# Plain FFN tiles: the down product in three stages, weight sums in place, rows as four chains, a planner with longer vector operations

## The chip, the cores and the metric

One core of a Trainium2 chip. The metric is the device time of one execution in microseconds (us), the median of three runs. Engines: PE (matmul), DVE (vector), ACT (activation), POOL (GpSimd), SP (issues most DMAs).

## The reference

One block of a network on x of 4096 positions by 640 features, in float32. Mod vectors come from a condition c; a spectral mixer works on the layer norm of x; then comes a gated feed-forward part on the layer norm of the result:

```python
mod = (_silu(c) @ w_mod).reshape(c.shape[0], 6, 1, -1)
h = _layernorm(x, axis=-1) * (1 + ca) + sa
x = x + ga * _A_ref(h, A_w1, A_b1, A_w2, A_b2)     # rfft, two small complex layers, soft threshold, irfft
h = _layernorm(x, axis=-1) * (1 + cb) + sb
x = x + gb * _B_ref(h, B_w_gate, B_w_up, B_w_down)  # (silu(h @ w_gate) * (h @ w_up)) @ w_down, 640 -> 1728 -> 640
```

## The kernel before

**Arithmetic.** To keep float32 accuracy, an operand is split into a high part (a rounded copy, ACT) and a low part (the rest, a subtraction on DVE), and a product is three matmuls: high by high, high by low, low by high.

**Phases.** The first 311 us are the mixer. What follows is the feed-forward part, over the 32 rows of 128 positions in six tiles (`TL`): two plain tiles of 4 rows (t = 0, 1) and four tiles of 6 rows (t = 2 to 5). The latter compute 2 x 2 blocks with seven products in place of eight (`seven`, `down7`); their sums of weights are made during the plain tiles and kept in DRAM (`td`, `wqd`).

**Stages of a plain tile.** The 1728 hidden features are six pairs of 256 (`NPR`), a half stage m and a small remainder s. `WG` lists the weight stages: g0, u0, s, g1, u1, g2, u2, ... g5, u5, m (gate and up of each pair), numbered n = 0 to 13. A weight stage is 30 matmuls of 128x512 into PSUM (`pg`). `down(t, p)` multiplies the hidden values (tiles `a`) by `w_down` (tiles `wq`) into PSUM banks `pd`, for each row g and half hf of the 640 features, and DVE adds each bank to the residual (`add_row`, the row L2246). The residual of tile 1 and later is loaded from DRAM (`x2d`).

**Weights.** `prep_w` splits gate and up weights (`r` to `wb`: high on ACT, low on DVE, in two pieces of 512 and 768 columns). `sum_w` makes the sums for the seven products (`ts` on POOL, `wt`, stored to `td`). `prep_wd` loads a pair of `w_down` (`wdr`, tag `wd`), multiplies it by the gate vector on POOL (L1483) and splits it (`wq`, low at L1494). `prep_wt` makes the four sums of the `w_down` blocks on POOL (`tr`), splits them (`tq`) and stores them. `kept_at(p)` names the plain tile in which pair p is also summed and stored.

**Rows.** Every row of tiles 1 to 5 has to be finished a tile ahead: load (`cr`, `x`, `gt`), gate product on POOL (L1610), split (`chh` on ACT, `chl` on DVE, L1617), a DFT product on PE (`py`, L1627), residual and statistics on DVE, scales on POOL, normed row on ACT (`xn`, L1658). Two rows make a pair: PE transposes them (`pt`, L1690), ACT scales, and the split result goes to DRAM (`ho` to `hs`).

**What sets the order.** All of this is planned when the kernel is built. Every operation is a `Step` with an engine, a reckoned duration, what it depends on, and the buffers it takes and frees; steps stand in chains. PE's matmuls are emitted in their order, and after every 0.3 us of them (`slot`) `sweep` tries each chain and emits the steps whose inputs are due by the planner's clock. `EARLY` says how far ahead of its due time a step may be emitted, and "T" is a step on PE (DFT product or transpose). What a stage needs and is not emitted yet, `until` and `force` emit at once. Each engine then works its queue strictly in that order. Durations reckoned for DVE's split of a `w_down` tile, for a weight sum and a row's split, and for POOL's gate product:

```python
Step("V", 0.83, lambda f=f: low(f), (("wdhh", t, p, f),), ("wdf", t, p, f),
Step("V", 0.7, low, (("tsh", n, i),), ("tsl", n, i), free=(tag,) if i else ()),
Step("V", 0.83, low, (k("chh"),), k("chl"), free=("pc",))
Step("P", 1.62, gated, (k("cr"),), k("crg"))
```

Of the kernel before, what the change touches and what calls it, by code (L numbers as in the profile page):

```python
# [173 lines left out]
def body(tc, x, w1, b1, w2, b2, wg, wu, wd, c, wm, k_fa, k_tb, k_tx, k_bm, k_bx, k_ga, k_ge, k_id, out, dbg=None):  # L174
# [27 lines left out]
    with ExitStack() as top:  # L202
# [836 lines left out]
        with ExitStack() as ff:  # L1039
# [22 lines left out]
            STG7 = [x for n, (k, p) in enumerate(WG) for x in [("w", n)] + [("d", p // 2 - 1)] * (k == "g" and p in (2, 4))]  # L1062
            STG7.append(("d", NPR // 2 - 1))

# [11 lines left out]
            LAT = 0.12  # L1076
            now = [0.0]
# [4 lines left out]
            EARLY = {"A": 0.0, "V": 0.3, "P": 0.3, "S": 0.3, "G": 0.3, "T": -1.5, "N": 0.0}  # L1082
# [5 lines left out]
            half1 = {"wd": 1, "wq": 4, "tr": 1, "tq": 2, "sg": 4, "hx": 5, "rb0": 1, "ra0": 1, "ra1": 1}  # L1088
# [9 lines left out]
            class Chain:  # L1098
# [11 lines left out]
                def at(self):  # L1110
                    st = self.steps[0]
                    t = 0.0
                    if st.e == "T" and not any(room[f"p{q}"] for q in (1, 2, 3)):
                        return None
                    for d in st.deps:
                        if d not in done:
                            return None
                        t = max(t, done[d])
                    for tag in st.use:
                        if not room.get(tag):  # L1120
                            return None
                        t = max(t, min(room[tag]))
                    return t

                def run(self):
# [10 lines left out]
                    elif e == "N":  # L1136
                        end = t
                    elif e in "SG":
                        q = "S" if e == "S" else "P"
                        issue = max(free[q], now[0], t) + (0.45 if e == "S" else 0.6)  # L1140
                        st.f()
                        free[q] = issue
                        free["D"] = max(free["D"], issue + 0.9) + 1.1 * st.n
                        end = free["D"] + 1.3
                    else:
                        start = max(free[e], now[0], t)
                        st.f()
                        free[e] = start + st.n
                        end = free[e] + LAT
# [35 lines left out]
            def sweep():  # L1185
                held = False
                for c in tails + chains:
                    if c in rows:

                        if held:  # L1190
                            continue
                        tries(c)
                        held = len(c.steps) > 0
# [12 lines left out]
            def force(c):  # L1206
                st = c.steps[0]
                for d in st.deps:
                    until(d)
                for tag in st.use:  # L1210
                    make_room(tag)
                c.run()

            def until(key):
                while key not in done:
                    force(owner[key])
# [3 lines left out]
            def make_room(tag):  # L1220
                while not room[tag]:
                    for c in tails + chains:
                        k = next((k for k, st in enumerate(c.steps) if tag in st.free), None)
                        if k is not None and (c.steps[k].e != "x"):
                            force(c)
                            break
                    else:
# [29 lines left out]
            def second_half():  # L1257
                nonlocal hq
                while tails:
                    while tails[0].steps:  # L1260
                        force(tails[0])
                    tails.pop(0)
                half.close()
                halves.pop(0)
                first.clear()
# [56 lines left out]
            def free_bank(qs):  # L1322
                while not any(room[f"p{q}"] for q in qs):
                    force(next(c for c in rows if c.steps and c.steps[0].e in "AV"))
# [11 lines left out]
            rows = [chain() for _ in range(NT)]  # L1336
# [129 lines left out]
            def kept_at(p):  # L1466
                return 0 if p < NPR // 2 else 1
# [4 lines left out]
            def prep_wd(t, p):  # L1472
# [15 lines left out]
                def high(f):  # L1488
                    wqs[t, p, f] = take("wq", [P, 2, 2, 320], F32R, 4, f"wq{t}_{p}_{f}")
# [29 lines left out]
            def prep_wt(p):  # L1519
                tr, tq = [], {}  # L1520

                def sub(j):
                    if j == 0:
                        tr.append(take("tr", [P, 4, 320], F32, 1, f"tr{p}"))
                    b11, b12, b21, b22 = (wdraw[p][:, f, 320 * e:320 * e + 320] for f in range(2) for e in range(2))
                    a, b = ((b12, b11), (b22, tr[0][:, 0]), (b22, b12), (b21, tr[0][:, 1]))[j]
                    pool.tensor_tensor(tr[0][:, j], a, b, op=OP.subtract)

                def high(i):
                    tq[i] = take("tq", [P, 2, 2, 320], F32R, 2, f"tq{p}_{i}")  # L1530
                    act.activation(tq[i][:, :, 0], tr[0][:, 2 * i:2 * i + 2], AF.Copy)

                def low(i):
                    dve.tensor_tensor(tq[i][:, :, 1], tr[0][:, 2 * i:2 * i + 2], f32(tq[i][:, :, 0]), op=OP.subtract)

                def store(i):
# [3 lines left out]
                            ("tr", p, j), ("tr",) if j == 0 else (), ("wd",) if j == 3 else ()) for j in range(4)]  # L1540
                for i in range(2):
                    out += [Step("A", 0.74, lambda i=i: high(i), (("tr", p, 2 * i), ("tr", p, 2 * i + 1)), ("tqh", p, i), ("tq",)),
                            Step("V", 0.83, lambda i=i: low(i), (("tqh", p, i),), ("tql", p, i), free=("tr",) if i else ()),
# [7 lines left out]
            DORD = ((1, 0), (2, 2), (6, 5), (7, 6), (5, 4), (4, 7), (3, 3))  # L1551
# [214 lines left out]
            def row_chain(t):  # L1766
# [157 lines left out]
            def finish0(t, n, f, pg):  # L1924
# [9 lines left out]
                else:  # L1934
                    tags, fc, sg = (f"a{2 * f}", f"a{2 * f + 1}"), 2 * p + f, sgs[f]
# [222 lines left out]
            def down(t, p):  # L2158
                G = 2 * TL[t][1]
                last = p == NPR - 1  # L2160
# [5 lines left out]
                for q in [p] + ([NPR] if last else []):  # L2166
# [3 lines left out]
                need(2 * p)  # L2170
                need(2 * p + 1)
# [6 lines left out]
                def seq(g, hf):  # L2178
                    q = []
                    for f in range(2):  # L2180
                        w = wqs[t, p, f]
                        l = [left(t, 2 * p + f, hl, g) for hl in range(2)]
# [12 lines left out]
                def put(g, hf, x):  # L2195
                    end = add_row(t, g, hf, x[0])
                    room[x[1]].append(end)
                    if last:
                        done["o", t, g, hf] = end

                def out(g):
                    H = TL[t][1]
                    outs.add([out_step(t, g, ("gx",) * ((g % H == H - 1) if t else 2 * (g == G - 1)))])

                for gs in ([(0, 1)] if last else [(0,)]) + [(g,) for g in range(2 if last else 1, G)]:
                    pd = {}
                    for g in gs:
                        for hf in range(2):
                            pd[g, hf] = any_bank(f"pd{t}_{p}_{g}_{hf}")
                            s = seq(g, hf)  # L2210
                            if last and len(gs) == 1:
                                s += tail_seq(g, hf)
                            for i, (l, m) in enumerate(s):
                                mm(pd[g, hf][0][:, :320], l, m, start=i == 0, stop=i == len(s) - 1 and not (last and len(gs) > 1))  # L2214
                            slot(0.147 * len(s))
                            if not last or len(gs) == 1:
                                put(g, hf, pd[g, hf])
                    if last and len(gs) > 1:
                        need(12)
                        for g in gs:  # L2220
                            for hf in range(2):
                                s = tail_seq(g, hf)
                                for i, (l, m) in enumerate(s):
                                    mm(pd[g, hf][0][:, :320], l, m, start=False, stop=i == 2)
                                slot(0.147 * 3)
                                put(g, hf, pd[g, hf])
                    if last:
                        for g in gs:
                            out(g)

                x = now[0] + 0.2
                for q in [p] + ([NPR] if last else []):
# [6 lines left out]
                for tag in ("a0", "a1", "a2", "a3") + (("ra0", "ra1", "rb0") if last else ()):  # L2239
# [165 lines left out]
            for t in range(NT):  # L2405
# [12 lines left out]
                if t:  # L2418
                    left_l.add(load_h(t))
                    x2_l.add(load_x2(t))  # L2420
                    rows[t].add(row_chain(t))

            for t in range(NT):

                for c in (sums, parts, down_s, down_t, outs):
                    chains.remove(c)
                    chains.insert(len(chains) - max(NT - 2 - t, 0), c)
                if t == NS:
                    second_half()
                for what, n in STG if t < NS else STG7:  # L2430
# [39 lines left out]
```

## Time and profile before

| | |
|---|---|
| median of 3 runs | 1451.06 us (1449.36 to 1453.6) |
| profiled execution | 1449.34 us, span 1447.5 us |
| PE, DVE, ACT, POOL busy | 97%, 75%, 53%, 41% of the span |
| DMA | 377.34 MB, mean 261 GB/s |

A row of the windows has the stretch, its length, then busy time and number of instructions of each engine, the clock that PE was granted (1.00 is full), and DMA. A row of the waits names who waited for whom, with the total, how often, and the longest. In the timeline a row has its start, its length and, in brackets, how long its engine was idle before and what ended that. A row of the groups has a line, the tiles written and read, the shape, the number of instructions, their busy time in us and the mean of one in ns, and the idle time before them. PE's matmuls overlap, so their own lengths say less than the distance of their starts.

### The profile page before, as it was taken

What the parts mean: (1) busy time and instruction counts of PE and PEld (TensorE: products, weight loads), DVE (VectorE), ACT (ScalarE), POOL (GpSimd) and SP (SyncE); (2) the same over time, 40 slices, a digit from 0 to 9 for tenths busy, and PEclk for the clock granted to TensorE, in tenths of its full rate; (3) what the DMA queues carried; (4) which work ended last, traced back from release to release, by engine and by line L of the source; (5) the groups of instructions that cost most, each with busy time, mean ns of one, the idle gap of its engine ahead of it and who ended that gap; (6) DMA issues with size and microseconds to landing.
All of it is one profiled execution on the core that took longest, in us unless ns stands there. A gap on an engine that the chain in (4) does not pass through costs nothing.

```text
span 1447.5 us, 23838 instructions
## 1 busy us (share of the span) xinstructions
PE 1397.2 (97%) x8410; PEld 1312.3 (91%) x8410; DVE 1079.9 (75%) x1911; ACT 763.7 (53%) x1542; POOL 591.5 (41%) x681
## 2 busy tenths in 40 slices
PE   7899999998999999999999999999999999999998
PEld 2599999967889888799999999999999999999998
DVE  8979888879988878838797757776667667365654
ACT  6779999744554444536454437354254535152441
POOL 5500200146756565515354625346334525052341
PEclk9999999999999999999999999999999999999999
DMA  9866466658976878998878997867997676955634
GB/s 366 312 213 213 157 196 208 205 170 268 324 251 222 306 236 295 320 387 302 289 241 288 325 357 259 284 228 262 384 326 246 238 279 243 361 178 198 219 126 145
DMA packets 170873, 377.34 MB, mean 261 GB/s; under 512 B 22178, under 2 KB 81634, under 8 KB 168739
## 3 DMA queue, kind: packets, MB, share of 16 engines
q1 hardware_dynamic: 161650, 359.28, 71.4%
q0 software_dynamic: 6800, 13.93, 2.9%
q10 hardware_dynamic: 2304, 2.62, 0.5%
q8 instruction: 66, 1.08, 0.3%
q14 instruction: 53, 0.43, 0.1%
HBM read 269.48 MB, written 96.80 MB: 253 GB/s over the span
## 4 chain that ended last, share of the span: by engine, by line
PE 59%; DVE 11%; issue 11%; DMA 8%; POOL 6%; ACT 3%; SPq 1%; DVEq 0%; POOLq 0%; ACTq 0%
PE pc L2289 8%; PE pw L1985 7%; PE pw L1987 7%; PE pw L1986 7%; PE pe L2289 6%; PE pd L2214 3%; DVE wb L1382 2%; PE pw L1996 2%; PE pw L1998 2%; PE pw L1997 2%; PE pc L707 2%; PE pl L657 2%; DMA h<-hs 2%; PE pg L1910 1%; PE pg L1908 1%
## 5 line engine op out<-in xcount | busy, mean ns | idle before, releaser
L1382 DVE TENSOR_TENSOR wb<-r,wb 128x768 fp32r<-128x768 f32 (+3 forms) x170 | 159.5, 949 | 11.3 <-ACT wb L1375 11.2
L1985 PE MATMUL pw<-h,wt 128*128 128x384 f32 x412 | 140.8, 342 | 6.9 <-ACT s_x L2004 3.8
L2045 POOL TENSOR_TENSOR sg<-s_x,sg 128x384 f32<-128x384 f32 x24 | 29.3, 1219 | 281.5 <-DVE s_x L2011 281.4
L1987 PE MATMUL pw<-h,wt 128*128 128x384 f32 x412 | 138.4, 336 | 0.0
L1986 PE MATMUL pw<-h,wt 128*128 128x384 f32 x412 | 138.1, 335 | 0.0
L2289 PE MATMUL pc<-wq,L 128*128 128x320 f32 x846 | 132.5, 310 | 1.2 <-DMA wq<-wqd 1.2
L2065 DVE TENSOR_TENSOR L<-sg,L 128x384 fp32r<-128x384 f32 x144 | 102.4, 732 | 39.2 <-ACT L L2061 35.3
L2289 PEld LDWEIGHTS pc<-wq,L 128*128 128x128 f32 x846 | 126.2, 188 | 1.8 <-DVE x L2246 1.2
L1375 ACT ACTIVATE wb<-r 128x768 fp32r<-128x768 f32 (+3 forms) x168 | 104.4, 637 | 43.7 <-PE pw L1998 39.5
L1910 PE MATMUL pg<-ht,wb 128*128 128x512 f32 x260 | 102.5, 394 | 5.5 <-DVE wb L1382 5.5
L1985 PE MATMUL pw<-h,wb 128*128 128x384 f32 x312 | 104.6, 335 | 0.0
L1987 PE MATMUL pw<-h,wb 128*128 128x384 f32 x312 | 104.4, 335 | 0.0
L1986 PE MATMUL pw<-h,wb 128*128 128x384 f32 x312 | 104.4, 335 | 0.0
L1908 PE MATMUL pg<-ht,wb 128*128 128x512 f32 x260 | 103.2, 397 | 1.2 <-ACT sg L1930 0.9
L2289 PE MATMUL pe<-wq,L 128*128 128x320 f32 x648 | 102.1, 310 | 1.5 <-DVE s_v L2011 0.8
L1909 PE MATMUL pg<-ht,wb 128*128 128x512 f32 x260 | 102.1, 393 | 0.0
L2004 ACT ACTIVATE s_x<-pw 128x384 f32<-128x384 f32 x52 | 25.4, 489 | 144.5 <-PE pw L1987 144.2
L2289 PEld LDWEIGHTS pe<-wq,L 128*128 128x128 f32 x648 | 96.3, 188 | 2.5 <-DVE s_v L2011 1.4
L2056 POOL TENSOR_TENSOR sg<-sg,sg 128x384 f32<-128x384 f32 x72 | 86.6, 1203 | 24.0 <-DVE L L2065 15.5
L2214 PE MATMUL pd<-wq,a 128*128 128x320 f32 x620 | 95.1, 310 | 0.0
L2214 PEld LDWEIGHTS pd<-wq,a 128*128 128x128 f32 x620 | 92.2, 188 | 1.0
L2246 DVE TENSOR_TENSOR x<-x,pc 128x320 f32<-128x320 f32 x144 | 68.2, 483 | 28.8 <-PE pc L2289 25.9
(324 smaller groups left out, 3892.9 us busy)
## 6 DMA issues: line engine op xcount, KB each, us to landing
wq<-wqd SPq DMA_DIRECT2D x83, 640.0 KB, 6.7
wt<-td SPq DMA_DIRECT2D x103, 512.0 KB, 4.9
hs<-ho SPq DMA_DIRECT2D x52, 512.0 KB, 6.1
h<-hs SPq DMA_DIRECT2D x32, 768.0 KB, 8.1
td<-wt SPq DMA_DIRECT2D x25, 512.0 KB, 5.1
r<-in_B_w_gate_dram SPq DMA_DIRECT2D x24, 384.0 KB, 4.6
r<-in_B_w_up_dram SPq DMA_DIRECT2D x24, 384.0 KB, 3.5
xx<-tt SPq DMA_DIRECT2D x56, 160.0 KB, 3.3
```

The costliest lines, as they stand in the source:

```text
L1375: def high(ks, e=slice(0, c), copy=lambda o, i: act.activation(o, i, AF.Copy)):
L1382: dve.tensor_tensor(wbs[t, n][:, 1, ks, e], raw[t, n][:, ks, e], f32(wbs[t, n][:, 0, ks, e]), op=OP.subtract)
L1908: mm(b, wh, hh, start=(kk == 0), stop=False)
L1909: mm(b, wh, hl, start=False, stop=False)
L1910: mm(b, wl, hh, start=False, stop=(kk == 4))
L1985: mm(b, w(0, kp), a[:, kp, 0], start=start and kp == 0, stop=False, skip_group_check=not start)
L1986: mm(b, w(0, kp), a[:, kp, 1], start=False, stop=False, skip_group_check=not start)
L1987: mm(b, w(1, kp), a[:, kp, 0], start=False, stop=kp == 1, skip_group_check=not start)
L2056: pool.tensor_tensor(o, x, y, op=op)
L2065: dve.tensor_tensor(o[:, 1], raws[j], f32(o[:, 0]), op=OP.subtract)
L2214: mm(pd[g, hf][0][:, :320], l, m, start=i == 0, stop=i == len(s) - 1 and not (last and len(gs) > 1))
L2289: mm(o[:, :320], ls[q][:, x, k], w[:, q, y], start=start and q == 0 and n == 0, stop=q == 1 and n == 2, skip_group_check=not start)
```

## The change

- `down` takes two pairs at a time: three stages per plain tile, after g2, after g4 and at the end, 12 products per bank (14 in the last stage, and 17 with the m part) in place of 6 (8, and 11).
- The sums in `prep_wt` are written over the loaded weights, so the tile `tr` goes. Buffers: `wd` 2 (was 1), `wq` 6 (was 4), `tq` 1 (was 2). The `hx` tiles of the start hold the hidden values of odd pairs.
- `kept_at`: pairs 3 to 5 are summed and stored in tile 0, pairs 0 to 2 in tile 1 (it was the other way round).
- The rows of a tile are four chains (pair steps, first rows, second rows, loads) in place of one.
- The planner multiplies durations on DVE and POOL by `SLOW`, except a row's residual adds and statistics: 1.3 and 1.2 in the plain tiles, 1.15 and 1.13 after. A "T" step is emitted once its input has been due for 0.5 us, it was 1.5. `force`, `until` and `make_room` go by one function `advance`, which emits what is possible and looks for what stands in the way.

```diff
-            STG = []
-            for n, (k, p) in enumerate(WG):
-                STG.append(("w", n))
-                if k == "g" and p:
-                    STG.append(("d", p - 1))
-            STG.append(("d", NPR - 1))
+            STG = [x for n, (k, p) in enumerate(WG) for x in [("w", n)] + [("d", p // 2 - 1)] * (k == "g" and p in (2, 4))]
+            STG.append(("d", NPR // 2 - 1))
...
+            SLOW = {"V": 1.3, "P": 1.2}
...
-            EARLY = {"A": 0.0, "V": 0.3, "P": 0.3, "S": 0.3, "G": 0.3, "T": -1.5, "N": 0.0}
+            EARLY = {"A": 0.0, "V": 0.3, "P": 0.3, "S": 0.3, "G": 0.3, "T": -0.5, "N": 0.0}
...
-            half1 = {"wd": 1, "wq": 4, "tr": 1, "tq": 2, "sg": 4, "hx": 5, "rb0": 1, "ra0": 1, "ra1": 1}
+            half1 = {"wd": 2, "wq": 6, "tq": 1, "sg": 4, "hx": 5, "rb0": 1, "ra0": 1, "ra1": 1}
...
-                        free[e] = start + st.n
+                        free[e] = start + st.n * (SLOW.get(e, 1.0) if st.key[0] not in ("x2", "mv") else 1.0)
...
+                SLOW.update(V=1.15, P=1.13)
...
-            rows = [chain() for _ in range(NT)]
+            rows = [[chain() for _ in range(4)] for _ in range(NT)]
+            tile_of = {c: t for t in range(NT) for c in rows[t]}
...
-                return 0 if p < NPR // 2 else 1
+                return 0 if NPR // 2 <= p < NPR else 1
...
-                    a, b = ((b12, b11), (b22, tr[0][:, 0]), (b22, b12), (b21, tr[0][:, 1]))[j]
-                    pool.tensor_tensor(tr[0][:, j], a, b, op=OP.subtract)
+                    o, a, b = ((b11, b12, b11), (b12, b22, b12), (b22, b22, b11), (b21, b21, b22))[j]
+                    pool.tensor_tensor(o, a, b, op=OP.subtract)
...
-                out = row_load(r0)
...
-                for i, (a, b) in enumerate(ab):
-                    (a1, a2), (b1, b2) = row_steps(a), row_steps(b)
-                    out += a1 + row_load(b) + a2[:4] + b1 + a2[4:] + b2
-                    st = pair_steps(t, i)
-                    m = 9
-                    out += st[:m] + (row_load(ab[i + 1][0]) if i + 1 < H else []) + st[m:]
-                return out
+                one, loads = ([], []), []
+                for i, rs in enumerate(ab):
+                    for h, r in enumerate(rs):
+                        c, x, g = row_load(r)
+                        if i:
+                            c.deps = tuple(("py", q, 1) for q in ab[i - 1])
+                        loads += [c, x, g]
+                        a1, a2 = row_steps(r)
+                        one[h].extend(a1 + a2)
+                return [[st for i in range(H) for st in pair_steps(t, i)], *one, loads]
...
-                need(2 * p)
-                need(2 * p + 1)
+                for f in range(4 * pp, 4 * pp + 4):
+                    need(f)
```

How the order moves on DVE in the opening of tile 0, between the products of stage u0 and the weights of stage g1 (`sg` the product with the gate, `a` the low hidden part, `wq` a split of `w_down`, `wb_3` the weights of g1, `x` the adds of a row's DFT product, `tq` the split of a sum). Before:

```order
L1940 TENSOR_TENSOR sg_0_0_4052<-pg_1_0_4165,sg_0_0_4052 128x512
L1494 TENSOR_TENSOR wq_0_0_4063<-wdr_0_4053,wq_0_0_4063 128x2x320
L1494 TENSOR_TENSOR wq_0_1_4219<-wdr_0_4053,wq_0_1_4219 128x2x320
L1945 TENSOR_TENSOR a_0_0_1_4057<-sg_0_0_4052,a_0_0_0_4056 128x512
L1940 TENSOR_TENSOR sg_0_1_4163<-pg_1_1_4208,sg_0_1_4163 128x512
L1382 TENSOR_TENSOR wb_3_4246<-r_3_4182,wb_3_4246 128x512
L1631 TENSOR_TENSOR x_4049<-x_4049,py_0_4258 128x320
L1631 TENSOR_TENSOR x_4049<-x_4049,py_1_4262 128x320
L1945 TENSOR_TENSOR a_0_1_1_4059<-sg_0_1_4163,a_0_1_0_4058 128x512
L1534 TENSOR_TENSOR tq_0_4269<-tr_4233,tq_0_4269 128x2x320
L1382 TENSOR_TENSOR wb_3_4246<-r_3_4182,wb_3_4246 128x768
```

And DVE's rows in the same place after:

```order
L1951 TENSOR_TENSOR sg_0_0_4052<-pg_1_0_4173,sg_0_0_4052 128x512
L1640 TENSOR_TENSOR x_4049<-x_4049,py_0_4214 128x320
L1640 TENSOR_TENSOR x_4049<-x_4049,py_1_4218 128x320
L1502 TENSOR_TENSOR wq_0_0_4063<-wdr_0_4053,wq_0_0_4063 128x2x320
L1956 TENSOR_TENSOR a_0_0_1_4057<-sg_0_0_4052,a_0_0_0_4056 128x512
L1502 TENSOR_TENSOR wq_0_1_4238<-wdr_0_4053,wq_0_1_4238 128x2x320
L1951 TENSOR_TENSOR sg_0_1_4171<-pg_1_1_4209,sg_0_1_4171 128x512
L1390 TENSOR_TENSOR wb_3_4258<-r_3_4199,wb_3_4258 128x512
L1390 TENSOR_TENSOR wb_3_4258<-r_3_4199,wb_3_4258 128x768
```

The two pieces of `wb_3` now follow each other; the adds stand ahead of them, `a_0_1` behind, and `tq_0` is gone from here.

PE at the first row's DFT product in tile 0 (`pg_1` is stage u0, `pg_2` stage s, `py` the DFT product). Before, it stood after the ninth matmul of stage s:

```order
L1908 MATMUL pg_2_0_4237<-ht_2_4043,wb_2_4178 128x512
L1909 MATMUL pg_2_0_4237<-ht_2_4043,wb_2_4178 128x512
L1910 MATMUL pg_2_0_4237<-ht_2_4043,wb_2_4178 128x512
L1627 MATMUL py_0_4258<-chh_4186,gt_4040 128x320
L1627 MATMUL py_0_4258<-chl_4187,gt_4040 128x320
L1627 MATMUL py_0_4258<-chh_4186,gt_4040 128x320
```

On PE after, it stands behind the third matmul of u0's second half:

```order
L1919 MATMUL pg_1_1_4209<-ht_3_4041,wb_1_4037 128x512
L1920 MATMUL pg_1_1_4209<-ht_3_4041,wb_1_4037 128x512
L1921 MATMUL pg_1_1_4209<-ht_3_4041,wb_1_4037 128x512
L1636 MATMUL py_0_4214<-chh_4188,gt_4040 128x320
L1636 MATMUL py_0_4214<-chl_4189,gt_4040 128x320
L1636 MATMUL py_0_4214<-chh_4188,gt_4040 128x320
```

It has moved 21 matmuls towards the start: the other 12 of that half and 9 of stage s now follow it.

More of the change, by code (lines that the diff above doesn't have):

```diff
@@ L1118, in at @@
                         t = max(t, done[d])
-                    for tag in st.use:
-                        if not room.get(tag):
+                    for tag in set(st.use):
+                        n = st.use.count(tag)
+                        if len(room.get(tag, ())) < n:
                             return None
-                        t = max(t, min(room[tag]))
+                        t = max(t, sorted(room[tag])[n - 1])
                     return t
@@ L1258, in second_half @@
                 nonlocal hq
[L1259 to L1262, printed above, removed]
+                for c in [*tails, sums, parts, down_s, down_t]:
+                    while c.steps:
+                        force(c)
+                tails.clear()
                 half.close()
                 halves.pop(0)
+                SLOW.update(V=1.15, P=1.13)
                 first.clear()
@@ L1323, in free_bank @@
                 while not any(room[f"p{q}"] for q in qs):
-                    force(next(c for c in rows if c.steps and c.steps[0].e in "AV"))
+                    force(next(c for c in tile_of if c.steps and c.steps[0].e in "AV"))
                 return min((q for q in qs if room[f"p{q}"]), key=lambda q: min(room[f"p{q}"]))
@@ L1934, in finish0 @@
                 else:
-                    tags, fc, sg = (f"a{2 * f}", f"a{2 * f + 1}"), 2 * p + f, sgs[f]
+                    tags, fc, sg = ("hx", "hx") if p % 2 else (f"a{2 * f}", f"a{2 * f + 1}"), 2 * p + f, sgs[f]
                 for q in tags:
@@ L2164, in need @@
                     wait_pe(done["act", t, f])
-                for q in [p] + ([NPR] if last else []):
+                for q in ps:
                     for key in wd_keys(t, q):
@@ L2193, in tail_seq, with go @@
                     return [(l[0], v[:, hf, 0]), (l[0], v[:, hf, 1]), (l[1], v[:, hf, 0])]
[L2195 to L2203, printed above, removed]
+                def go(b, s, start, stop):
+                    for i, (l, m) in enumerate(s):
+                        mm(b[:, :320], l, m, start=start and i == 0, stop=stop and i == len(s) - 1)
+                        if i % 6 == 5:
+                            slot(0.147 * 6)
+                    slot(0.147 * (len(s) % 6))
                 for gs in ([(0, 1)] if last else [(0,)]) + [(g,) for g in range(2 if last else 1, G)]:
+                    part = last and len(gs) > 1
                     pd = {}
@@ L2238, in down @@
                             room["wq"].append(x)
-                for tag in ("a0", "a1", "a2", "a3") + (("ra0", "ra1", "rb0") if last else ()):
+                for tag in ("a0", "a1", "a2", "a3") + ("hx",) * 4 + (("ra0", "ra1", "rb0") if last else ()):
                     room[tag].append(x)
@@ L2420, in body @@
                     x2_l.add(load_x2(t))
-                    rows[t].add(row_chain(t))
+                    for c, steps in zip(rows[t], row_chains(t)):
+                        c.add(steps)
             for t in range(NT):
-                for c in (sums, parts, down_s, down_t, outs):
+                for c in (sums, parts, down_s, outs):
                     chains.remove(c)
-                    chains.insert(len(chains) - max(NT - 2 - t, 0), c)
+                    chains.insert(len(chains) - 4 * max(NT - 2 - t, 0), c)
                 if t == NS:
                     second_half()
-                for what, n in STG if t < NS else STG7:
+                for what, n in STG:
                     if what == "d":
```

115 lines of the change are left out of this document (59 added, 56 removed).

## The prediction

> **What bounds the kernel now.** I read the page first, then the windows, then PE's own waits by stage, then the timeline at the longest of them.
>
> ```profile
> span 1447.5 us, 23838 instructions
> PE 1397.2 (97%) x8410; PEld 1312.3 (91%) x8410; DVE 1079.9 (75%) x1911; ACT 763.7 (53%) x1542; POOL 591.5 (41%) x681
> ...
> core 0: us, PE busy (x) PEld busy (x) DVE busy (x) ACT busy (x) POOL busy (x), PEclk, DMA share, GB/s
> 326.00:352.00 26.00, 21.44 (x85) 16.55 (x86) 24.01 (x26) 13.08 (x24) 19.13 (x16) 0.87 0.78 255
> 342.00:349.00 7.00, 4.26 (x11) 3.12 (x11) 6.24 (x6) 3.18 (x6) 5.77 (x4) 0.53 0.60 182
> 352.00:476.00 124.00, 123.92 (x688) 111.47 (x687) 110.00 (x164) 62.98 (x110) 76.64 (x80) 1.00 0.80 274
> 476.00:634.00 158.00, 150.00 (x795) 131.86 (x794) 125.71 (x193) 71.85 (x128) 86.55 (x89) 1.00 0.85 299
> 634.00:1444.00 810.00, 797.45 (x4865) 787.87 (x4862) 543.74 (x957) 355.71 (x765) 330.11 (x335) 1.00 0.76 266
> ```
>
> PE sets the end, and the change leaves every matmul in place. So it can only take PE's gaps away, or add some. The five windows are the opening of tile 0, a half-clock stretch in it, the rest of tile 0, tile 1, and tiles 2 to 5. PE is idle for 26 − 21.44 = 4.6 us, 0.1, 8.0 and 12.6 us in the four that do not overlap: 25.2 us together. The half clock adds (1 − 0.53) × 7 = 3.3 us, of which a part lies under the wait named next. About 27 us, 1.9% of the span, is therefore the most that a new order can bring. Who keeps PE waiting (columns: in total, times, longest), in the opening, in tiles 0 and 1 after it, the three longest of tiles 2 to 5:
>
> ```profile
> PE pg L1910 <- DVE wb L1382: 4.1, 2, 2.7
> ...
> PE pt L1690 <- ACT xn L1658: 3.7, 2, 3.0
> PE py L1627 <- issue: 1.9, 1, 1.9
> PE pg L1910 <- DVE wb L1382: 1.4, 1, 1.4
> PE pd L2224 <- DVE a L1945: 0.8, 1, 0.8
> ...
> PE pw L1985 <- ACT s_x L2004: 3.8, 4, 2.0
> PE pw L1985 <- ACT s_v L2004: 1.5, 4, 0.6
> PE pw L1985 <- ACT s_y L2004: 1.3, 4, 0.5
> ```
>
> **Tile 0's opening.** Stage g1 of tile 0 (gate, pair 1) waits for the low part of its weights, `wb_3`. On DVE there stood, between the two pieces of it:
>
> ```profile
> 339.24 0.68 DVE L1382 TENSOR_TENSOR wb<-r,wb 128x512 fp32r<-128x512 f32 x1
> 339.84 0.87 DVE L1631 TENSOR_TENSOR x<-x,py 128x320 f32<-128x320 f32 x2
> 340.64 1.77 DVE L1945 TENSOR_TENSOR a<-sg,a 128x512 fp32r<-128x512 f32 x1
> 342.33 1.34 DVE L1534 TENSOR_TENSOR tq<-tr,tq 128x640 fp32r<-128x640 f32 x1
> 343.59 1.47 DVE L1382 TENSOR_TENSOR wb<-r,wb 128x768 fp32r<-128x768 f32 x1
> ```
>
> In the changed order both pieces are neighbours, the `tq` step has gone to pairs 3 to 5, and the `a` step stands behind. That takes 1.77 + 1.34 = 3.1 us from in front of the second piece (the two `x` adds stay ahead of it, only earlier), more than its wait of 2.7 us. One sum of weights (`wt_01`) also moves behind and the adds come in front, so the first piece is not later. I take the whole 4.1 us as gone. The wait overlaps the half clock: in 342 to 349 PE is busy for 4.26 us at 0.53, which costs 4.26 × 0.47 = 2.0 us. That goes too, if the waits caused it: −6.1 us.
>
> [...]
>
> Against it, the first DFT product `py` now stands 21 matmuls earlier on PE (shown with the change). Neighbouring matmuls start 0.23 us apart:
>
> ```profile
> 330.05 2.19 DVE L1617 TENSOR_TENSOR chl<-cr,chh 128x640 fp32r<-128x640 f32 x1
> ...
> 335.73 0.30 PE L1627 MATMUL py<-chh,gt 128*128 128x320 f32 x1
> ...
> 426.12 0.39 PE L1908 MATMUL pg<-ht,wb 128*128 128x512 f32 x1
> 426.35 0.40 PE L1909 MATMUL pg<-ht,wb 128*128 128x512 f32 x1
> ```
>
> Its input was ready at 332.24, 3.5 us ahead of its use. 21 × 0.23 = 4.8 us earlier means that PE waits 1.3 us; the input itself may come a little sooner or later (one `wb` step has moved in front of it). I take +1.5, between 0 and 2.5. Opening: −4.6 us.
>
> **Down in three stages.** The matmuls stay; half of the adds into the residual go.
>
> ```profile
> L2246 DVE TENSOR_TENSOR x<-x,pd 128x320 f32<-128x320 f32 x96 | 42.9, 475 | 7.6 <-DMA x<-x2d 3.9 <-PE pd L2214 3.5
> ...
> 513.92 0.49 DVE L2246 TENSOR_TENSOR x<-x,pd 128x320 f32<-128x320 f32 x1 [3.89 <-DMA x<-x2d]
> ...
> 515.91 0.38 PE L1627 MATMUL py<-chh,gt 128*128 128x320 f32 x1 [1.94 <-issue]
> ```
>
> 48 adds × 0.475 = 23 us less on DVE in 308 us of tiles 0 and 1. DVE is busy there for 0.80 to 0.92 of the time, beside PE, so this by itself is worth nothing; it gives room. But tile 1's first add waited 3.9 us for its residual `x2d`, held PSUM banks meanwhile, and PE stood still for 1.9 us. The first down stage now comes two weight stages later: 60 matmuls × 0.23 = 13.8 us, far past the 3.9. −1.9 us. In the last stage the four held banks take 14 products each ahead of the remainder, before 8, so the wait of 0.8 us for `a12` is covered: −0.8 us. The wider stages need `wq` and `a` buffers for two pairs; there are six `wq`, and the `hx` tiles serve the odd pairs. Nothing waits longer for these by the order.
>
> **Weight sums in place, two `wd` buffers.** The four subtractions, two splits and two stores per pair stay, on all their queues. What goes is the wait for a single `wd` buffer. The longest wait of tile 1 came from it:
>
> ```profile
> 576.40 3.56 POOL L1483 TENSOR_TENSOR wdr<-wdr,gbb 128x640 f32<-128x640 f32 x2 [4.72 <-DMA wdr<-in_B_w_down_dram]
> ...
> 581.37 0.92 ACT L1658 ACTIVATE xn<-x,nm_b,rs_b 128x640 f32<-128x640 f32 x1 [6.72 <-POOL nm_b L1649]
> 582.34 0.55 PE L1690 MATMUL pt<-idn,xn 128*128 128x128 f32 x3 [3.02 <-ACT xn L1658]
> ```
>
> POOL waited for the load with a row's scales queued behind. With a load ahead this should shrink; but the buffer is now also held until the last split. I take −2.0 of the 3.0, between 0 and −3.0. Pairs 0 to 2 are now prepared for storing in tile 1 and 3 to 5 in tile 0, so tile 1's opening gets what tile 0's loses. Its `wb` wait of 1.4 us stays, and I add 1.0 (0 to 3).
>
> **Four chains, the planner's longer operations, transposes nearer.** The planner now reckons 1.3 for DVE in tiles 0 and 1 (1.15 later) and lets PE come at 0.5 in place of 1.5 after an input is due. The first is closer to the trace: `wq` is entered at 0.83, `wt` at 0.70.
>
> ```profile
> L1494 DVE TENSOR_TENSOR wq<-wdr,wq 128x640 fp32r<-128x640 f32 x28 | 31.2, 1142 | 2.0 <-ACT wq L1490 1.8
> L1617 DVE TENSOR_TENSOR chl<-cr,chh 128x640 fp32r<-128x640 f32 x28 | 30.2, 1077 | 7.7 <-ACT chh L1614 7.7
> L1449 DVE TENSOR_TENSOR wt<-ts,wt 128x512 fp32r<-128x512 f32 x25 | 27.0, 1081 | 9.8 <-ACT wt L1445 9.8
> ```
>
> 1142/830 = 1.38, 1081/700 = 1.54, and `chl` 1077/830 = 1.30. The second takes 1.0 us of slack from each of 28 rows' DFTs and 14 transposes. What slack there was, once each in tiles 0, 2 and 4:
>
> ```profile
> 389.78 1.36 DVE L1617 TENSOR_TENSOR chl<-cr,chh 128x640 fp32r<-128x640 f32 x1
> 391.10 0.30 PE L1627 MATMUL py<-chh,gt 128*128 128x320 f32 x1
> ...
> 735.08 0.81 DVE L1617 TENSOR_TENSOR chl<-cr,chh 128x640 fp32r<-128x640 f32 x1
> 736.63 0.31 PE L1627 MATMUL py<-chh,gt 128*128 128x320 f32 x1
> ...
> 1127.15 0.82 DVE L1617 TENSOR_TENSOR chl<-cr,chh 128x640 fp32r<-128x640 f32 x1 [1.71 <-ACT chh L1614]
> 1130.00 0.31 PE L1627 MATMUL py<-chh,gt 128*128 128x320 f32 x1
> ```
>
> That is 0.0, 0.7 and 2.0 us. So a row in tiles 0 and 1 would wait a whole us longer, if nothing else changed; but its planned steps have grown as well, `chl` by 0.25, the gate product on POOL (entered at 1.62, factor 1.2) by 0.32, so about half is given back, and DVE is freer. I take +2.0 for the 18 places there (−2 to +9) and −1.0 for tiles 2 to 5 (−6 to +6): the waits for ACT's evacuations come from ACT stuck behind late inputs, which the truer factors should thin, while nearer products give some back.
>
> Sum: −4.6 − 1.9 − 0.8 − 2.0 + 1.0 + 2.0 − 1.0 = −7.3 us. The profiled execution took 1449.34 us (1447.5 of it span), so 1442.0; it stood 1.72 below the median of the three runs, so the time is **1443.8 us**.
>
> **The rivals.**
> - *Larger gain.* The truer factors also clear the ACT waits of tiles 2 to 5 (3.8 + 1.5 + 1.3 = 6.6) and the rows cost nothing (−2.0): 1443.8 − 6.6 + 1.0 − 2.0, so about 1436. For it: those waits are the largest there. Against: they fall beside `rest` and the keeping copies, whose order hardly moves.
> - *No change.* Half of the 12 us of removed waits returns elsewhere on DVE, as the same work stands before the same deadlines: tile 1's opening (3.0) and the rows (4.0) take back the 7: 1451.
> - *Slower.* The split rows and nearer products make row inputs the bound: with two rows at once on POOL and DVE, each of 42 places waits 0.5 us more than counted. +21 − 7.3 = +13.7, so about 1465. It decides from 7.3/42 = 0.17 us per place on. For it: the slack of 0.0 above. Against: 2.0 in the late tiles, and 23 us less on DVE.
>
> **How the numbers follow.** Forecast 0.43, larger gain 0.20, no change 0.19, slower 0.18. The forecast's own range is 1438 to 1448. A measurement of this kernel can tell about 0.3% (4.4 us) from no change. Faster by more, below 1446.7: the first two less the forecast's upper end, plus the lower end of no change, 0.62; slower by more, above 1455.4: 0.18; within: 0.20. The range of 1431 to 1461 takes in three cases and the near half of the slower one.
>
> **What would show it.** After: no `wb` wait over 1 us in tile 0's opening, and a granted clock of 1.00 at 342 to 349; no wait of the add for `x2d`; 48 adds; a wait of about 1.5 us at the first `py`. It is wrong if PE's waits on `chl` and `xn` add up to more than 10 us, or if the opening of tile 1 loses over 4.

## The result, and the profile after

The changed kernel takes 1433.89 us (median of four runs, 1431.21 to 1435.43) beside 1450.72 of the kernel before: a ratio of 0.988, 95% interval 0.986 to 0.990. The forecast was 1443.8, with a range of its own of 1438 to 1448: the direction was right, and the gain of 7.3 us was too small by about 10, so that the time lies below that range, nearest to the 1436 of the rival of the larger gain. The profiled executions differ by 18.1 us.

The head of the page after:

```profile
span 1429.4 us, 23767 instructions
PE 1389.7 (97%) x8410; PEld 1313.1 (92%) x8410; DVE 1061.5 (74%) x1863; ACT 762.1 (53%) x1542; POOL 594.9 (42%) x681
```

And the windows of the same stages. At 326.2 us the kernel before starts stage u0, and the changed one the last two products of g0. From there the borders have moved, tile 1 is now 475 to 623.5 and tiles 2 to 5 are 623.5 to 1426:

```profile
326.00:352.00 26.00, 23.47 (x105) 19.12 (x106) 23.23 (x30) 15.42 (x26) 12.83 (x12) 1.00 0.52 175
342.00:349.00 7.00, 6.18 (x28) 4.86 (x28) 6.51 (x8) 4.74 (x8) 5.14 (x4) 1.00 0.49 171
352.00:475.00 123.00, 121.51 (x675) 109.05 (x674) 105.46 (x143) 63.86 (x111) 90.27 (x90) 1.00 0.89 311
475.00:623.50 148.50, 148.20 (x796) 131.78 (x795) 113.59 (x163) 73.37 (x132) 84.25 (x85) 1.00 0.90 316
623.50:1426.00 802.50, 794.75 (x4858) 789.26 (x4856) 542.21 (x955) 350.52 (x758) 328.24 (x332) 1.00 0.77 265
```

PE's idle time in these four stretches was 25.2 us and is 2.5 + 1.5 + 0.3 + 7.8 = 12.1. Nearly all of tile 1's 8.0 is gone. The other 5 us lie in PE's busy time. The half clock of 342 to 349 is gone (0.53 before, 1.00 now), but tiles 2 to 5 have one of 3.4 us that they did not have (shown at the end), so the clock's share of the 5 us is small: by estimate 4.26 × 0.47 = 2.0 us went and 3.40 × 0.50 = 1.7 us came. The rest is pace: products follow each other a little closer (busy time over matmuls in tile 1: 148.20/796 = 0.186 us, before 150.00/795 = 0.189), and why is not read off here. Who keeps PE waiting now, in the opening (two rows), the rest of tile 0, tile 1, and tiles 2 to 5:

```profile
PE py L1636 <- DVE chl L1626: 2.3, 2, 1.5
PE pg L1871 <- DVE ht L1858: 1.2, 1, 1.2
...
PE py L1636 <- DMA gt<-in_k_ga_dram: 0.9, 1, 0.9
...
PE pt L1699 <- ACT xn L1667: 0.3, 1, 0.3
...
PE pw L1996 <- ACT s_x L2015: 2.1, 2, 1.3
PE pe L2333 <- DMA wq_-1_11807<-wqt: 2.0, 1, 2.0
PE pe L2333 <- DMA wq_-1_9451<-wqt: 1.4, 1, 1.4
PE pc L2293 <- DVE s_v L2022: 0.9, 1, 0.9
```

The opening's waits on `wb` are gone. The longest left there is the first DFT product's, on its `chl`, as the timeline shows (two rows of PE, then two of DVE); the two `wb` pieces of stage g1, at 337.78, now follow each other:

```profile
326.20 0.73 PE L1871 MATMUL pg<-ht,wb 128*128 128x512 f32 x2 [1.22 <-DVE ht L1858]
...
333.24 0.42 PE L1636 MATMUL py<-chl,gt 128*128 128x320 f32 x1 [1.51 <-DVE chl L1626]
...
331.85 1.34 DVE L1626 TENSOR_TENSOR chl<-cr,chh 128x640 fp32r<-128x640 f32 x1
...
337.78 1.61 DVE L1390 TENSOR_TENSOR wb<-r,wb 128x512 fp32r<-128x512 f32 x2
```

And the group of the adds of the plain tiles, 48 in place of 96, with no wait for `x2d` left:

```profile
L2250 DVE TENSOR_TENSOR x<-x,pd 128x320 f32<-128x320 f32 x48 | 22.6, 481 | 15.8 <-PE pd L2209 15.8
```

### The profile page after: what moved, and what is told of

Same layout as the page of the kernel before. It is cut to its first block, busy times and chain, and to the rows that moved or that the text cites. A ratio compares the mean times of both kernels' runs of the same rounds, so it can differ in the third digit from the quotient of the medians.

```text
span 1429.4 us, 23767 instructions
## 1 busy us (share of the span) xinstructions
PE 1389.7 (97%) x8410; PEld 1313.1 (92%) x8410; DVE 1061.5 (74%) x1863; ACT 762.1 (53%) x1542; POOL 594.9 (42%) x681
## 4 chain that ended last, share of the span: by engine, by line
PE 68%; DVE 3%; DMA 3%; issue 1%; ACT 1%; POOL 1%; SPq 0%; DVEq 0%; ACTq 0%; POOLq 0%
PE pw L1996 8%; PE pw L1998 8%; PE pw L1997 8%; PE pc L2293 8%; PE pe L2293 6%; PE pd L2209 6%; PE pg L1921 3%; PE pg L1919 3%; PE pg L1920 3%; PE pw L2009 2%; PE pw L2007 2%; PE pw L2008 2%; PE py L1636 2%; PE pf L2333 1%; PE pt L1699 1%
## 5 line engine op out<-in xcount | busy, mean ns | idle before, releaser
L2076 DVE TENSOR_TENSOR L<-sg,L 128x384 fp32r<-128x384 f32 x144 | 105.9, 753 | 30.7 <-ACT L L2072 29.9
L764 POOL DMA_DIRECT2D s<-co x28 | 15.5, 553 | 179.4 <-ACT co L763 179.4
```

Source lines behind the costliest of these rows:

```text
L2076: dve.tensor_tensor(o[:, 1], raws[j], f32(o[:, 0]), op=OP.subtract)
```

## Experiments

Ratios are to the kernel before on the same chips, with 95% intervals. Waits are those of PE.

### One part of the change undone

Planning factors off, everywhere (both edits) and in tiles 2 to 5 alone (the second edit):

```diff
-            SLOW = {"V": 1.3, "P": 1.2}
+            SLOW = {"V": 1.0, "P": 1.0}
-                SLOW.update(V=1.15, P=1.13)
+                SLOW.update(V=1.0, P=1.0)
```

> The changed kernel with the planner's factors back at 1.0 in both halves; all else stays. Theory P (the gain beyond the forecast comes from the truer durations, which place every step): most of the 17 us goes, 1444 to 1452 us, tile 1 longer by 5 us or more and tiles 2 to 5 by 4 or more. Theory W (it comes from the wide down stages and the room they give DVE in the plain tiles): 1433 to 1438. Theory C (the split row chains): 1433 to 1438.

> The changed kernel with the factors of the second half (tiles 2 to 5) at 1.0; tiles 0 and 1 keep 1.3 and 1.2 and their order. Theory P (truer durations bring the gain of tiles 2 to 5): plain tiles as after, tiles 2 to 5 longer by 7 us or more, 1441 or more, with the waits for ACT's evacuations back at 5 to 7 us. Rival L (tiles 2 to 5 gained by where the loads of the next tile's left operand happen to fall on SP's queue, not by the factor): no more than 4 us in those waits; the time moves only if waits on h appear.

Measured: 1469.7 us, 1.012 (1.010 to 1.014), and 1451.2, 0.999 (0.997 to 1.001). The waits after 320 us of the first:

```profile
PE py L1636 <- DVE chl L1626: 11.0, 7, 2.9
PE py L1636 <- DMA gt<-in_k_ga_dram: 8.6, 3, 4.6
```

And those of the second in tiles 2 to 5:

```profile
PE py L1636 <- DVE chl L1626: 7.6, 3, 3.5
PE pw L1996 <- ACT s_x L2015: 2.8, 3, 1.6
```

So the rows' products do come too early for their inputs when T is -0.5 and the durations are short: the slower rival's mechanism exists (11.0 + 8.6 = 19.6 us in the first run), and the factors are what keeps it away. In the second run the order of the plain tiles is that of the changed kernel, instruction by instruction, and the loss lies in tiles 2 to 5, which take 820.2 us in place of 802.4:

```profile
625.90:1446.10 820.20, 799.17 (x4857) 790.71 (x4856) 545.40 (x954) 352.68 (x758) 327.01 (x332) 1.00 0.74 259
```

Its waits for ACT's evacuations are 3.6 us there (2.8 on `s_x`, 0.8 on `s_v`), not the 5 to 7 that I expected.

T back at -1.5, and, in another run, one row chain per tile in place of four (its steps in their old sequence):

```diff
-... "T": -0.5,
+... "T": -1.5,
```

```diff
-            rows = [[chain() for _ in range(4)] for _ in range(NT)]
+            rows = [[chain()] for _ in range(NT)]
```

> The changed kernel with products of rows emitted 1.5 us after their input is due, as before, in place of 0.5. My prediction's term (the nearer products cost 2 us in the plain tiles and about nothing later): 1430 to 1433, a little faster than the changed kernel. Rival (rows that are ready earlier release the queues behind them, the nearer products are part of the gain): 1436 to 1442.

> The changed kernel with the rows of a tile as one chain again. Theory C (rows that run side by side stop queues from waiting for one row's loads and statistics): 1440 to 1450, with waits for the transposes' input back in tile 1. Theories P and W: 1433 to 1437.

Measured: 1454.1, 1.001 (0.999 to 1.002), and 1501.1, 1.035 (1.033 to 1.037). With T -1.5 the longest of PE's waits is

```profile
PE pw L2007 <- DMA h<-hs: 10.1, 2, 7.4
```

and in the timeline of SP, ahead of tile 3, the last load of `h` stands behind two `wq` loads that came 8 us after the issue before them:

```profile
837.34 0.80 SPq L1565 DMA_DIRECT2D wq<-wqd  x2
838.18 1.36 SPq L1808 DMA_DIRECT2D h<-hs  x1
```

With one chain PE waits, around the start of tile 2 (two rows, 641 us) and of tile 3 (880 us), for

```profile
PE pw L1994 <- DMA h<-hs: 26.1, 4, 11.4
PE pw L2005 <- DMA h<-hs: 7.0, 1, 7.0
...
PE pw L2005 <- DMA h<-hs: 11.3, 1, 11.3
```

Both lose at the border of two tiles, where the next tile's normed rows (`h`) are not loaded in time.

Down in six stages again (with four `wq` and two `tq` buffers):

> The changed kernel with the down product of the plain tiles in six stages again (wq 4, tq 2 buffers as before, wd 2, sums in place). Theory W: 1441 to 1450, tile 1 longer by 5 us or more, the wait of the adds for the loaded residual back (2 to 4 us), tiles 2 to 5 as after. Theories P and C: 1434 to 1438 (my two small terms, 1.9 and 0.8 us, come back).

Measured: 1454.4, 1.002 (1.001 to 1.003); waits of 5.8 us on `h` and 6.2 on `wb`. DVE's wait for `x2d` is back, 5.3 us, and PE waits 1.3 us behind these adds:

```profile
L2252 DVE TENSOR_TENSOR x<-x,pd 128x320 f32<-128x320 f32 x96 | 43.0, 478 | 16.5 <-PE pd L2211 10.9 <-DMA x<-x2d 5.3
```

Each part undone thus brings the time to that of the kernel before or above it, though their single terms in the prediction are 0 to 2 us; four of these five runs took longer than any range that I expected of them. That fits no sum of terms: either the parts need each other, or any change of the order costs what this order happens to save.

### The same kernels with the order drawn anew

One number of the planner moved by a hundredth re-draws the order without touching the work: `LAT`, the latency added to each step's end (0.12 in both kernels), or the factors of tiles 2 to 5 by 0.01, which leaves the order of the plain tiles as it is.

```diff
-            LAT = 0.12
+            LAT = 0.13
```

> The changed kernel with the second half's factors at 1.16 and 1.14 in place of 1.15 and 1.13: a nudge with no meaning, which moves some orders. Theory P: 1432 to 1437, since the durations are as true as before. Rival L: the time may move by 5 to 15 us either way, all of it in tiles 2 to 5 at the borders between tiles.

> The changed kernel with the planner's latency between engines at 0.13 in place of 0.12 us: a nudge of all tiles. If the gain belongs to the parts of the change: 1430 to 1438. If a part of it is where orders happen to fall: 1438 to 1455.

> The kernel before with the same nudge of the planner's latency, 0.13 in place of 0.12 us. If the kernel before is typical of its planner: 1447 to 1455. If its time is an accident of order as well: outside of that.

> The changed kernel with the planner's latency at 0.11 us. With 0.12 it took 1433.9 and with 0.13 1444.8. If the shown time is a lucky draw of a spread: 1436 to 1450. If 0.13 was the unlucky one: 1430 to 1436.

> The kernel before with the planner's latency at 0.11 us. With 0.12 it took 1451 to 1452, with 0.13 1481.5. If the shown time of before is a lucky draw: 1456 to 1485, with waits on h at the tile borders. If 0.13 was the exception: 1447 to 1456.

> The changed kernel with the planner's latency 0.14. Theory R: the rows of tile 3 end over 60 us ahead of its start, as in every draw of the changed kernel so far (68 to 77), no wait on h over 5 us, 1434 to 1452 us. If the 1433.9 of the shown order is a lucky draw, this one lies at 1443 to 1452 as 0.11 and 0.13 did; if it is typical, at 1434 to 1440.

> The kernel before with the planner's latency 0.14. Theory R: one chain leaves the rows' lead to the draw: either the lead of tile 3 is about 60 us and the time 1448 to 1456 (as with 0.11 and 0.12), or it is under 20 us and the time 1470 to 1485 (as with 0.13). Nothing between them. Rival D: time and lead go separate ways, so a time over 1465 with a lead over 50.

| order | before, us | ratio | changed, us | ratio |
|---|---|---|---|---|
| LAT 0.11 | 1451.5 | 0.999 (0.997 to 1.000) | 1450.9 | 0.999 (0.997 to 1.001) |
| LAT 0.12, as shown | 1450.7 | 1 | 1433.9 | 0.988 (0.986 to 0.990) |
| LAT 0.13 | 1481.5 | 1.021 (1.019 to 1.022) | 1444.8 | 0.995 (0.994 to 0.997) |
| LAT 0.14 | 1478.0 | 1.018 (1.015 to 1.020) | 1446.8 | 0.996 (0.994 to 0.999) |
| LAT 0.12, factors +0.01 | | | 1437.5 | 0.992 (0.990 to 0.994) |

All ratios are to the kernel before in its own order. The changed kernel's shown order is the best of its five. The mean of its four ratios over LAT is 0.9946, or 1443 us on the scale of the kernel before. With LAT 0.11 the two kernels do not differ; with 0.13 and 0.14 they differ by 37 and 31 us, mostly by what the kernel before loses (next section). Tile 1 shows what differs among the changed kernel's orders. In each of three other orders of the changed kernel, the window of it and then the longest of PE's waits in it. LAT 0.11:

```profile
484.20:639.80 155.60, 150.65 (x796) 133.63 (x795) 120.33 (x163) 73.31 (x132) 84.08 (x85) 0.98 0.89 307
```

```profile
PE py L1636 <- DVE chl L1626: 4.7, 1, 4.7
```

LAT 0.13:

```profile
473.90:630.00 156.10, 150.99 (x802) 133.80 (x800) 122.22 (x173) 74.85 (x136) 87.81 (x92) 0.99 0.89 305
```

```profile
PE pg L1921 <- DVE wb L1390: 3.5, 2, 2.6
```

LAT 0.14:

```profile
471.80:627.20 155.40, 149.67 (x800) 132.17 (x800) 122.23 (x172) 74.81 (x134) 85.27 (x90) 1.00 0.86 301
```

```profile
PE pt L1699 <- ACT xn L1667: 3.6, 2, 1.9
```

Three orders, three operands that come late, 5 to 6 us of idle PE each; the shown order has 0.3. The work of the whole kernel is the same.

### Why the kernel before loses 30 us in two of four orders

With LAT 0.13 and 0.14 the kernel before waits 25 us for `h`, at the starts of tiles 3 and 4. In SP's timeline of the kernel before, the last store of tile 3's rows (`hs`) and the first loads of `h` behind it:

```profile
779.15 0.62 SPq L1735 DMA_DIRECT2D hs<-ho  x1
802.04 1.36 SPq L1797 DMA_DIRECT2D h<-hs  x2
```

The same with LAT 0.13, and in PE's the wait that follows:

```profile
835.26 0.38 SPq L1735 DMA_DIRECT2D hs<-ho  x1
840.41 4.66 SPq L1797 DMA_DIRECT2D h<-hs  x6
...
859.59 0.69 PE L1996 MATMUL pw<-h,wb 128*128 128x384 f32 x1 [17.57 <-DMA h<-hs]
```

Tile 3 starts at 841.5 and 839.7. So the rows were done 62 us ahead of it in the one order, and 4 us ahead in the other (5 with LAT 0.14): one chain takes its three row pairs one after the other, and where the first pair comes some 40 us later (first store at 657 and 696), the third ends at the border. What delays the first pair stays open. Two tests. If SP's order were to blame, loading `h` ahead of the other loads, and without the planner's limit on waiting DMA work, would mend it:

```diff
-            gate, prep, wld, wtl, down_w, left_l, x2_l, sums, ... = [chain() ...]
+            gate, prep, left_l, wld, wtl, down_w, x2_l, sums, ... = [chain() ...]
```

> The nudged kernel before (latency 0.13, 1481.5 us), with the loads of the next tile's left operand tried ahead of the weight loads and without their limit on planned DMA work. Rival L (the nudge cost its 29 us at the tile borders, because those loads stand behind others on SP's queue): the 25.6 us of PE's waits on h fall below 5, 1450 to 1460. Otherwise (the rows are late, the loads only show it): 1470 or more, the wait stays on the stores of hs.

> The changed kernel with the same earlier loads of the left operand. It had no wait on h, so by rival L nothing is to be gained: 1431 to 1438, unless the weight loads behind come late (waits on wq of 2 to 5 us more, 1436 to 1440).

Measured: 1483.1, 1.019 (1.017 to 1.021), no better. Its longest waits:

```profile
PE pw L1996 <- DMA h<-hs: 19.8, 2, 18.2
PE pc L2289 <- DMA wq<-wqd: 11.3, 2, 7.5
```

The changed kernel gets worse by it, 1460.2, 1.004 (1.003 to 1.006), since the loads of `wq` now stand behind:

```profile
PE pc L2293 <- DMA wq<-wqd: 22.2, 3, 8.0
```

If SP's order were the cause, the first would have come to 1450 to 1460; it is not the cause there. If the single row chain is, four chains will mend it. They were put into the kernel before, with what the planner needs for them and nothing else of the change:

> The kernel before, with one part of the change alone: the rows of a tile as four chains in place of one. Theory R (four chains finish the rows of the next tile earlier, so that its lefts are there when it opens; this is the change's own gain, and a part of the 17 us): 1440 to 1450 us, no wait on h over 2 us, the last store of tile 3's rows over 62 us ahead of tile 3's start (62 in the kernel before, 77 in the changed one). Rival D (the parts gain only together, since each re-draws the order): 1452 to 1475, with waits of 3 to 11 us on chl that the slower planning factors would have taken away, as in the runs without those factors.

> The kernel before with the planner's latency 0.13 and four chains in place of one. With one chain and 0.13 the time was 1481.5 us, with 25.6 us of waits on h, and the last store of tile 3's rows was only 4 us ahead of tile 3's start. Theory R: the rows are early again, over 50 us ahead, the waits on h fall under 6 us, and the time is 1446 to 1462. Rival Q (SP's queue holds the loads of h): the waits on h stay over 15 us and the time is over 1470.

Measured: 1457.3, 1.002 (1.000 to 1.004), and at LAT 0.13 1453.8, 1.002 (1.000 to 1.004). In SP's timeline at LAT 0.13, the last store of tile 3's rows, and then the wait on `h`:

```profile
748.77 0.36 SPq L1747 DMA_DIRECT2D hs<-ho  x1
```

```profile
PE pw L2010 <- DMA h<-hs: 1.8, 1, 1.8
```

Tile 3 starts at 857.9 there, 109 us behind the store, and 28 us of the time are back. So for LAT 0.13 the late rows of one chain are shown as the cause of that loss, and four chains as a cure; with 0.14 the cure was not run. In the five orders of the changed kernel, all with four chains, the lead of tile 3's rows is 51 to 77 us (for LAT 0.14 I had expected over 60; it is 51). But where the rows were early anyhow, four chains alone gain nothing: the 1440 to 1450 of the first theory was wrong, and the rival's waits came, 6.4 us on `chl` and `gt`.

### The two halves

All of the planner's part (four chains, factors, T) in the kernel before, and all of it undone in the changed kernel:

> The kernel before with the whole planner's half of the change (four row chains, the slower planning factors, T -0.5) and the old work: down in six stages, one wd buffer, weight sums in tiles of their own, old places of the stored blocks. If the planner's half is what took the late operands away, the waits on chl and gt of the run with four chains alone (6.4 us) fall under 3 us and the time is 1440 to 1452. If the parts gain only together with the new stages, as the run with six stages in the changed kernel says (1454.4), it is 1452 to 1458.

> The changed kernel with the planner's half undone (one row chain, no planning factors, T -1.5): the new stages and the weight sums in place alone. If one chain is the risk (44.6 us of waits on h in the changed kernel with one chain and the other planner's parts kept), the time is 1470 to 1510 with waits on h over 15 us; if it was the clash of one chain with the new factors, 1445 to 1455 with waits on h under 6 us.

Measured: 1453.0, 1.002 (1.000 to 1.004), and 1455.7, 1.002 (1.000 to 1.004). With the planner's half alone the waits on `chl` are down to 1.0 us, but PE waits (after 320 us) for `h`, `wb` and `wq`:

```profile
PE pw L2012 <- DMA h<-hs: 6.2, 2, 4.0
PE pg L1926 <- DVE wb L1396: 3.7, 2, 3.2
PE pd L2230 <- DVE wq L1508: 2.0, 2, 1.0
...
PE pd L2230 <- ACT wq L1504: 1.7, 1, 1.7
```

With the stages alone it waits for `xn`, `chl` and `wb`:

```profile
PE pt L1699 <- ACT xn L1667: 4.7, 4, 2.1
PE py L1636 <- DVE chl L1626: 4.4, 4, 2.6
PE pg L1919 <- DVE wb L1390: 2.8, 4, 1.1
```

In the run without the planner's half `h` waits only 0.7 us. So one chain is not late in every order; beside the new factors it cost 1501 us in the one order that was run. Neither half gains in the order that it got; the two together gain 0.4 to 1.2% in four of the five orders run, and in the fifth (LAT 0.11) nothing that can be told from noise. No version run beats the changed kernel.

## Why the prediction was right in direction and wrong in size

Against its own terms, from 326 us on (a border is the first product of a tile):

| stretch | forecast | measured |
|---|---|---|
| opening of tile 0 | -4.6 | -4.5: 20 more matmuls between 326 and 352, at 23.47/105 = 0.22 us |
| rest of tile 0 | about +1 (half of the rows' +2.0) | +3.5: 1.4 of waits, 7 more matmuls (1.6), rest unassigned |
| tile 1 | -1.9 - 0.8 - 2.0 + 1.0 + 1 = -2.7 | -9.0: 157.3 to 148.3 |
| tiles 2 to 5 | -1.0 | -7.9: 810.3 to 802.4 |

- **Opening: right.** No `wb` wait, clock 1.00 at 342 to 349, and 1.51 us at the first `py` where +1.5 was taken; a second wait on `chl` there adds 0.8. The half clock went with the waits, so the sum was right to count its 2.0 us. The start of tile 0 came 1.7 us earlier and that was lost again to `ht` (1.2 on DVE, 1.2 on ACT).
- **x2d and a12: right in this order.** The waits of 3.9 (DVE), 1.9 and 0.8 us are gone, and with six stages in the changed kernel the one on `x2d` is back (5.3). In the kernel before with four chains, or with the planner's half, which have six stages too, it is not there: this wait hangs on the order as well.
- **Tile 1: the step that failed, by its size.** I kept its `wb` wait of 1.4, took 2.0 of 3.7 us on `xn`, and added 1.0 for the opening and 1 for the rows. In the shown order of these only 0.3 us on `xn` is left: PE's idle time fell by 7.7 of 8.0, and the pace gave 1.3 more, together 6.3 us beyond the forecast. With LAT 0.11, 0.13 and 0.14 tile 1 takes 155.4 to 156.1, a gain of 1.2 to 1.9 where I forecast 2.7. With the factors 0.01 higher it is 148.3 again, but that is the same order of the plain tiles run once more and no further draw.
- **Tiles 2 to 5: the other one.** Forecast -1.0, from -6 to +6. The waits on ACT fell from 6.6 to 2.3, those on `h` (1.3) went; PE's waits there fell by 4.7 in all (12.3 to 7.6), and the rest is pace and a few matmuls less in the stretch (4858, before 4865). That the ACT waits would fall is what the rival of the larger gain (1436) said, which I gave 0.20. Its cause, the truer factors, is not shown: without them in these tiles the ACT waits are 3.6, still 3.0 less than before. What the factors do there is keep the rows' inputs in time (without them 7.6 on `chl`), and the tiles take 820.2 without them. The reason against the rival, that the order there "hardly moves", was wrong: rows, loads and copies are placed anew. With LAT 0.11, 0.13 and 0.14 these tiles take 805.7, 809.7 and 807.8: gains of 4.6, 0.6 and 2.5.
- **Slower: its mechanism was real, its condition was not met.** Without the factors the rows' inputs cost 19.6 us. With them `chl` and `xn` cost 3.1 (2.8 and 0.3), far from the 10 that would have refuted me.

So the reasons named were sound for what could be read off the order, and what made the gain 17 instead of 7 is the order's own fit in tiles 1 to 5. Over neighbouring orders the changed kernel lies at 1434 to 1451, the kernel before at 1451 to 1482. That the former lie around the forecast does not bear out its terms: in each of the three other orders tile 1 gains less than was forecast. What stays open: four values of one planner's number are not a random sample, and no run says which single placement frees tile 1 in the shown order. That weight sums in place and the second `wd` buffer matter by themselves was not run.

## What to carry to other kernels

When a planner writes the order, one run of a change measures the change and one draw of the order; move a number that should not matter by a hundredth, in both kernels, before crediting the change. A part's worth in such a kernel isn't its own: products brought nearer need truer durations. Read how far ahead an input is finished, not only how long it is waited for: the kernel before had 62 us of lead in its row chain in one order and 4 in the next, and its waits showed the danger only there.

## What the runs showed of the hardware

In the changed kernel a wait of 1.98 us for one load was followed by 3.4 us at a granted clock of 0.50. By an estimate from these two numbers, 3.40 × (1 − 0.50), that cost 1.7 us more, nearly as much again as the wait. PE's timeline, then the windows:

```profile
1025.60 0.74 PE L2333 MATMUL pe<-wq_-1_11807,a 128*128 128x320 f32 x2 [1.98 <-DMA wq_-1_11807<-wqt]
```

```profile
1025.80:1029.20 3.40, 3.40 (x14) 3.40 (x14) 0.97 (x2) 0.00 (x0) 0.00 (x0) 0.50 1.01 411
```

With the wait of 17.6 us (842.0 to 859.6) in the kernel before at LAT 0.13, the granted clock was 1.00 up to 847, 0.51 from there to 859.5, and 0.50 until 863.9, four microseconds into the work:

```profile
842.00:847.00 5.00, 0.02 (x1) 0.00 (x0) 0.00 (x0) 0.00 (x0) 0.69 (x2) 1.00 1.03 414
847.00:859.50 12.50, 0.00 (x0) 0.00 (x0) 0.00 (x0) 0.00 (x0) 0.00 (x0) 0.51 1.02 415
859.50:863.90 4.40, 4.31 (x13) 4.31 (x14) 0.56 (x1) 1.02 (x2) 0.00 (x0) 0.50 0.29 115
```

Length alone did not decide it here: the wait of 1.98 us was followed by a clock of 0.50, while in tile 1 of the kernel before PE waited 3.02 us, until 582.34, and the clock granted from there to 589.2 us was 1.00.

The loads of `h` with LAT 0.13 took from 840.4 to 859.6 us, with the DMA engines full (share 1.03 and 1.02) in the windows from 842 to 859.5. Six loads of 768 KB went out at once there, within 5 us. That is 4.7 MB, beside the 7.3 MB that 414 and 415 GB/s make in those windows; in the order with early rows the issues of `h` for tile 3 are spread from 802 to 834 us. At this border the late rows made their loads come all at once.
